# Mamba-2 scan and maxout FFN: seven products for block one's output, C of chunk two by VectorE, sign words by GpSimd, and a new order of the first steps

## The chip, the core and the metric

The kernel runs on one core of a Trainium2 chip. Its engines are TensorE (PE in the profile, its weight loads PEld), VectorE (DVE), ScalarE (ACT), GpSimd (POOL) and SyncE (SP), which issues the DMAs. Each works through its own queue in order; they wait for each other by semaphores. The metric is the device time of one execution in microseconds.

## What is computed

A Mamba-2 scan over 4 batches, 8 heads and 768 tokens (x of 32 per head, state of 16), whose output of 3072 tokens x 256 goes through a maxout feed-forward layer:

```python
for c in range(nc):                      # scan, per batch and head
    cum = np.cumsum(log(a[chunk]))
    L = np.exp(cum[:, None] - cum[None, :]) * causal
    y[chunk] = ((C @ B.T) * L) @ x + (C @ state) * np.exp(cum)[:, None]
    state = np.exp(cum[-1]) * state + (B * np.exp(cum[-1] - cum)[:, None]).T @ x
x = y.transpose(0, 2, 1, 3).reshape(3072, 256)
h = np.maximum(np.maximum(x @ w1, x @ w2), x @ w3)      # 256 x 768 each
out = h @ w_out                                         # 768 x 256
```

The weights come in float64, everything else in float32. The kernel uses chunks of 128 tokens where the reference has 32; the length of a chunk does not enter what is computed.

## The kernel before

**Blocks.** The 768 tokens are six chunks of 128. A chunk with its four batches makes a block of 512 token rows, c = 0 to 5. The text of the change counts from one: its block one is c = 0, its chunk three c = 2. For each block TensorE makes scores (C times B), VectorE multiplies them with the decays L, TensorE makes y from them and from the state, and the feed-forward layer follows.

**Feed-forward.** With w2 as base, h = x w2 + max(x(w1-w2), x(w3-w2), 0). The base part of the output is x G with G = w2 w_out, which is folded once (`fold_base`). For c > 0 the products of x with the weight differences, and those of h and x with w_out and G, are made by seven products in place of eight on halves of the operands (Strassen's way): `early_products` and `late_products` for the first, `down_seven` with `piece`, `first_four`, `all_seven` for the output. Seven products need sums and differences of the operands: of the weights (`weight_sums`, GpSimd), of y (`scan_sums`, VectorE), of h (`sums_of_h`, GpSimd, four instructions for a third of the rows), of w_out and G (`sums_of_out`, GpSimd). Block c = 0 uses plain products: `group` for x times the differences, `first_down` for the output, 16 steps of two matmuls 128x256. An fp32 matmul stands as two records in the profile.

**Weights.** Twelve pieces of 512 KB (nine of w1, w2, w3, three of w_out) are loaded as words of float64 and turned into float32 by hand. `decode_abs`: two ScalarE instructions, with the absolute value of the high words u put in SBUF ("dA") or in a PSUM bank ("dB"). `decode_bits`: three VectorE instructions (clamp L208, shift L211, join with the sign bit L213). `decode_sum`: GpSimd adds the low part (L220).

**Loads.** SP issues all large loads in the order of the steps. C of chunks three to five and B of the last are in `LONG`: eight loads of 32 KB with long runs, turned by four VectorE transposes (`turn_long`, L145) into SBUF. The other B and C are one load of 256 KB, turned by four TensorE transposes (L462) into a PSUM bank.

**Order.** `ORDER` is a list, written by hand, of named steps, up to the point where block c = 1 is nearly done; each engine gets its instructions in that order. After it a fixed plan (`STEADY`, `LAST`) runs blocks two to five. The names that matter here (c chunk, j piece, n and k counts):

- f: load of the next weight piece; lx, lB, lC, lL, lE: loads of x, B, C, L (half of the decays, 1 MB), E (eight rows); cs: store of the running sums; l3: all loads of chunk three
- dA, dB, dV, dP: decoding of piece j (ScalarE, VectorE, GpSimd); v: difference of weights (VectorE, L692); u: `weight_sums` (GpSimd)
- i, j, X: decays of chunk zero (TensorE, ScalarE); k, x: masks (GpSimd, L427) and exponentials (ScalarE, L434) of a later chunk; n, N: turning of sums to columns
- pB, pC: transposes of B, C; bB, c: copies of them (ScalarE); E, d: C times exp(cum), `scan_cd`; s: scores; w: scores times decays (VectorE, L556); o, y, Y: y from state, y from scores, copy; S: `scan_sums`; D, A, Z, z: the state
- g, G, H: x times the differences for block zero, and what follows; T, t, F, Fc: G folded
- e, ea, ev, K, Ko, Km, Kp: block one's (c = 1) early products, copy, sums, late products, their sums, maximum, `sums_of_h`
- O, Oc: `first_down`, and its copy and store; Sw, So: `sums_of_out` of w_out and of G

PSUM banks are shared: `att_bank` has four and takes every fifth from the one of sumA; `ffn_bank` has one and shares two of sumB. A step that asks for a bank waits until the last reader of the old content is through.

Of the kernel before, what the change touches and what calls it, by code (L numbers as in the profile page):

```python
# [19 lines left out]
def kernel(  # L20
# [20 lines left out]
    nc = tc.nc  # L41
# [3 lines left out]
    P = 128  # L45
# [76 lines left out]
    LONG = {(c, "C") for c in range(3, NC)} | {(NC - 1, "B")}  # L122
# [82 lines left out]
    def decode_bits(j):

        dst, hi, u, v, r = jobs[j]
        nc.vector.tensor_scalar(  # L208
            out=u.bitcast(FP32), in0=u.bitcast(FP32), scalar1=SMALL, scalar2=LARGE,
            op0=ALU.max, op1=ALU.min)  # L210
        nc.vector.tensor_scalar(  # L211
            out=u, in0=u, scalar1=3, scalar2=None, op0=ALU.logical_shift_left)
        nc.vector.scalar_tensor_tensor(  # L213
            out=v, in0=hi, scalar=0x80000000, in1=u,
            op0=ALU.bitwise_and, op1=ALU.bitwise_xor)

    def decode_sum(j):

        dst, hi, u, v, r = jobs[j]
        nc.gpsimd.tensor_tensor(  # L220
            out=dst.bitcast(U32), in0=v.rearrange("p (k f) -> p k f", k=2),
            in1=r.rearrange("p (k f) -> p k f", k=2), op=ALU.add)
# [706 lines left out]
    def down_seven(c, u, p):  # L929

        if p == EARLY[0]:
            open_seven(c, u, ffn_bank)
# [15 lines left out]
    def first_down(j):  # L948

        b, part = divmod(j, 4)  # L950
        u, i = divmod(b, 2)
        if j % 8 == 0:
            held["o"] = bank("ffn", 1, [P, 2, DM], "o")
        o = held["o"]
        for f in (2 * part, 2 * part + 1):
            if f < NF:
                one, two = hT[0][:, f, b * P:(b + 1) * P], wo_sb[:, f]
            else:
                one, two = yT[0][:, f - NF, b * P:(b + 1) * P], based["G"][:, f - NF]
            nc.tensor.matmul(  # L960
                out=o[:, i], lhsT=one, rhs=two, start=(f == 0), stop=(f == NF + KD - 1),
                skip_group_check=True)

    def first_out(u):
        ob = ffn.tile([P, 2, DM], FP32, tag="ob", bufs=2, name="ob")
        nc.scalar.copy(out=ob, in_=held["o"])
        nc.sync.dma_start(
            out=out.rearrange("(b s) m -> s b m", s=S)[0:P, 2 * u:2 * u + 2], in_=ob)
# [21 lines left out]

    step("tB", turn_rows, 0, "B")
# [16 lines left out]
    for c in range(3):  # L1008
        step("pB%d" % c, scan_tb, c, att_bank if c else pin("ffn"))
        step("bB%d" % c, scan_bt, c)  # L1010
        step("pC%d" % c, scan_tc, c, att_bank if c else pin("sumA"))
# [204 lines left out]
    for j in range(4 * NB):  # L1216
        step("O%d" % j, first_down, j)
    step("Oc0", first_out, 0)
    step("Oc1", first_out, 1)
# [4 lines left out]
        i0 ca fa tB pB0 bB0 tC j0 la X00 X01 ra pC0 c00 X11 f0 f1 lx0 f2 f3 c01 X10 s00 w001 w000  # L1224
        dA0 dA1 dV1 i2 j2 X20 dV0 n2 dP0 X21 s02 cs w002 w003 X31 f4 X30 w020 y00 Y00 w022 lB1 f5 f6
        n1 dP1 v0 g00 lL10 dA2 dB3 f7 f8 w021 w023 y02 Y02 dV2 f9 g10 dP2 lC1 lE1 N2 g01 H0 dV3 T0
        g11 dB4 lL12 dB5 dP3 v1 dV4 dV5 f10 f11 lx1 H1 t0 dP4 v2 pB1 N1 dB6 dB7 g20 g21 g30 dV6 D0
        lB2 fb bB1 dP5 k11 dP6 g31 G4 H3 H4 A0 G5 H2 dB8 H5 T1 t1 v3 n3 G6 G7 pC1 lC2 k10 x10 dV7
        dP7 dV8 v4 G8 H6 dP8 x11 N3 dA9 dV9 c10 E1 d1 G9 H7 Z0 H8 U k12 c11 s10 v5 x12 x13 G10 H9
        w100 dB10 w102 x14 dP9 w103 G11 s12 w101 k13 T2 x15 dV10 F0 u2 lL20 w120 D1 lE2 x16 x17 o1  # L1230
        w121 y10 y11 w122 alone u0 w123 y13 dP10 H10 u3 y12 A1 u5 u1 Y10 Y11 t2 H11 F1 S10 S11 S12
        S13 e0 lx2 pC2 Z1 ea0 ev0 pB2 dB11 K0 lL22 bB2 z1 dV11 dP11 Ko0 l3 c20 e1 ea1 ev1 O0 K1 E2
        k21 F2 Fc d2 Sw c21 Ko1 Km1 e2 k20 k23 ea2 O1 O2 ev2 K2 Ko2 s20 e3 x20 x21 k22 x22 x23 k30
        O3 O4 w203 O5 O6 O7 ea3 ev3 u4 w200 K3 x24 k31 x25 Oc0 Ko3 e4 ea4 So O8 Km3 O9 ev4 w201 O10
        K4 x30 x26 k33 Ko4 x27 O11 O12 w202 s22 w221 e5 w222 w223 w220 x31 x32 Kp1 x33 o2 y23 y20
        y21 y22 k32 Y20 Y21 S20 ea5 S21 O13 O14 O15 D2 ev5 Kp3 A2 Z2 K5 S22 S23 Ko5 x34 Oc1
# [125 lines left out]
```

## Time and profile before

| | |
|---|---|
| median of 3 runs | 256.97 us (256.96 to 257.55) |
| the profiled execution, whole | 257.36 us |
| its span in the profile | 255.6 us |
| granted TensorE clock | 0.999 |
| busy: PE, PEld, DVE, ACT, POOL | 247.3, 206.5, 172.7, 113.9, 107.2 us |
| read from and written to HBM | 24.54 MB, 3.24 MB |

The profile is one execution. Times of instructions count from the first one of the span. A PE record's end is modelled and overlaps the next one, so TensorE is read by the steps between starts. "<-" after an idle time names what ended it. In the table by stage each engine has its busy time and its count of instructions.

Landing times of loads, in us, as the issues of the trace have them: first two weight pieces 9.3 and 10.9, x of chunk zero 14.2, third piece 16.9; halves of L for chunk one 28.9 and 45.7; the eight rows E of chunk one 36.5 to 40.0; x of chunk one 52.0; C of chunk two 58.6.

### The profile page before, as it was taken

What the parts mean: (1) busy time and instruction counts of PE and PEld (TensorE: products, weight loads), DVE (VectorE), ACT (ScalarE), POOL (GpSimd) and SP (SyncE); (2) the same over time, 40 slices, a digit from 0 to 9 for tenths busy, and PEclk for the clock granted to TensorE, in tenths of its full rate; (3) what the DMA queues carried; (4) which work ended last, traced back from release to release, by engine and by line L of the source; (5) the groups of instructions that cost most, each with busy time, mean ns of one, the idle gap of its engine ahead of it and who ended that gap; (6) DMA issues with size and microseconds to landing.
All of it is one profiled execution on the core that took longest, in us unless ns stands there. A gap on an engine that the chain in (4) does not pass through costs nothing.

```text
span 255.6 us, 5657 instructions
## 1 busy us (share of the span) xinstructions
PE 247.3 (97%) x2172; PEld 206.5 (81%) x2172; DVE 172.7 (68%) x362; ACT 113.9 (45%) x308; POOL 107.2 (42%) x144
## 2 busy tenths in 40 slices
PE   8799899999999999999999999999999999999995
PEld 5357554588888887888899898898889899999994
DVE  4589998777627456588566688567877746645651
ACT  3837689845396844535164434354431211111010
POOL 2032682898949941661271470363230404134000
PEclk9999999999999999999999999999999999999999
DMA  3998968986995676868004925501000001001003
GB/s 107 240 295 235 344 88 205 232 99 178 199 299 130 93 109 169 234 81 137 4 0 129 256 62 97 80 3 41 3 13 29 3 0 44 0 3 41 1 15 110
DMA packets 85371, 28.16 MB, mean 110 GB/s; under 512 B 55392, under 2 KB 82016, under 8 KB 85344
## 3 DMA queue, kind: packets, MB, share of 16 engines
q1 hardware_dynamic: 84752, 27.40, 49.2%
q8 instruction: 17, 0.28, 0.5%
q10 hardware_dynamic: 592, 0.39, 0.5%
q14 instruction: 10, 0.08, 0.1%
HBM read 24.54 MB, written 3.24 MB: 109 GB/s over the span
## 4 chain that ended last, share of the span: by engine, by line
PE 82%; DVE 9%; issue 3%; POOL 2%; SPq 1%; DMA 1%; ACT 1%; POOLq 0%; DVEq 0%
PE o L886 25%; PE sumB L717 20%; PE sumA L717 16%; PE o L960 5%; PE s L548 5%; PE y L584 4%; PE fold L822 2%; PE y L571 2%; DVE w_u L213 2%; DVE u L211 2%; DVE u L208 1%; SPq L230 1%; DVE w L692 1%; DVE L L556 1%; DMA stage<-in_C_dram 1%
## 5 line engine op out<-in xcount | busy, mean ns | idle before, releaser
L434 ACT ACTIVATE L<-L,ncums 128x128 f32<-128x128 f32 x160 | 49.4, 392 | 3.4 <-POOL L L427 3.4
L556 DVE TENSOR_TENSOR L<-s,L 128x512 f32<-128x512 f32 x48 | 30.8, 682 | 10.6 <-ACT L L434 4.8
L717 PE MATMUL sumA<-yT,w 128*128 128x256 f32 x120 | 36.8, 388 | 0.0
L717 PE MATMUL sumB<-yT,rb 128*128 128x256 f32 x120 | 35.8, 380 | 0.0
L845 POOL TENSOR_TENSOR rb<-h 128x256 f32<-128x256 f32 x16 | 11.7, 730 | 56.9 <-DVE h L792 56.3
L745 ACT COPY eu<-sumA 128x256 f32<-128x256 f32 x30 | 11.2, 373 | 54.0 <-PE sumA L717 54.0
L427 POOL TENSOR_SCALAR_AFFINE_SELECT L<-L 128x1024 f32<-128x1024 f32 x20 | 21.6, 1092 | 9.1 <-DMA L<-cums 9.1
L717 PEld LDWEIGHTS sumB<-yT,rb 128*128 128x128 f32 x120 | 22.6, 190 | 3.5 <-issue 0.3
L656 PE MATMUL up<-yT,w 128*128 128x256 f32 (+1 forms) x64 | 23.0, 497 | 1.4 <-ACT yT L607 0.5
L717 PEld LDWEIGHTS sumA<-yT,w 128*128 128x128 f32 x120 | 19.4, 190 | 4.2 <-DVE rb L779 1.0
L755 DVE TENSOR_TENSOR eu<-sumA,eu 128x256 f32<-128x256 f32 x30 | 12.7, 422 | 13.7 <-ACT eu L745 13.6
L220 POOL TENSOR_TENSOR w<-w_u,w_r 128x512 uint32<-128x512 uint32 x9 | 12.5, 1392 | 20.6 <-DVE w_u L213 20.6
L845 POOL TENSOR_TENSOR w<-h 128x256 f32<-128x256 f32 x12 | 8.7, 729 | 28.0 <-DVE h L792 27.5
L656 PEld LDWEIGHTS up<-yT,w 128*128 128x128 f32 x64 | 11.3, 189 | 8.9 <-issue 5.3
L717 PE MATMUL sumA<-ys,rb 128*128 128x256 f32 x60 | 17.8, 379 | 0.0
L717 PE MATMUL sumB<-ys,w 128*128 128x256 f32 x60 | 17.8, 379 | 0.0
L717 PE MATMUL sumB<-ys,rb 128*128 128x256 f32 x60 | 17.8, 379 | 0.0
L548 PE MATMUL s<-CT,BT 32*128 32x256 f32 x192 | 15.8, 402 | 2.1 <-ACT CT L485 1.8
L886 PE MATMUL o<-rb,h 128*128 128x128 f32 x120 | 17.7, 275 | 0.0
L886 PE MATMUL o<-wo,h 128*128 128x128 f32 x120 | 17.6, 275 | 0.0
L779 DVE TENSOR_TENSOR m<-sumB,eu 128x512 f32<-128x512 f32 x15 | 10.3, 688 | 9.5 <-PE sumB L717 9.5
L548 PEld LDWEIGHTS s<-CT,BT 32*128 32x128 f32 x192 | 9.9, 184 | 7.2 <-ACT CT L485 2.8
(148 smaller groups left out, 516.2 us busy)
## 6 DMA issues: line engine op xcount, KB each, us to landing
L<-cums SPq DMA_DIRECT2D x10, 1024.0 KB, 8.8
rb<-in_moe_w_dram SPq DMA_DIRECT2D x9, 512.0 KB, 7.0
raw_x<-in_x_dram SPq DMA_DIRECT2D x6, 512.0 KB, 5.3
out_dram<-ob SPq DMA_DIRECT2D x10, 256.0 KB, 2.5
rb<-in_moe_w_out_dram SPq DMA_DIRECT2D x3, 512.0 KB, 8.3
E<-cums SPq DMA_DIRECT2D x40, 32.0 KB, 4.0
raw_B<-in_B_dram SPq DMA_DIRECT2D x4, 256.0 KB, 6.1
raw_C<-in_C_dram SPq DMA_DIRECT2D x24, 32.0 KB, 1.9
```

Source lines behind the costliest of these rows:

```text
L220: nc.gpsimd.tensor_tensor(out=dst.bitcast(U32), in0=v.rearrange("p (k f) -> p k f", k=2), in1=r.rearrange("p (k f) -> p k f", k=2), op=ALU ...
L427: nc.gpsimd.affine_select(out=Ls[c][:, b], in_=Ls[c][:, b], pattern=[[0, NH], [1, P]], compare_op=ALU.is_ge, fill=MASKED, base=0, channel_ ...
L434: nc.scalar.activation(L[:, b, h], L[:, b, h], AF.Exp, bias=ncum[c][:, b * NH + h:b * NH + h + 1], scale=1.0)
L548: nc.tensor.matmul(out=s[:, i].rearrange("j g i -> j (g i)"), lhsT=st["BT"][rows, b], rhs=st["CT"][rows, b].rearrange("p g i -> p (g i)"), ...
L556: nc.vector.tensor_tensor(out=M, in0=s, in1=M, op=ALU.mult)
L656: nc.tensor.matmul(out=bank[:, a:b], lhsT=w_sb[i][:, k, f * P:(f + 1) * P], rhs=yT[0][:, k, a:b], start=(k == 0), stop=(k == KD - 1), skip ...
L717: nc.tensor.matmul(out=bank[:, half], lhsT=left(p, k), rhs=sides[c][p], start=(first and half == 0), stop=True, skip_group_check=True)
L745: nc.scalar.copy(out=eu[:, 0], in_=units[c, k][0][:, 0])
L755: nc.vector.tensor_tensor(out=eu[:, 1], in0=A[:, 1], in1=eu[:, 0], op=ALU.add)
L845: eng.tensor_tensor(out=to, in0=a1, in1=a0, op=ALU.subtract)
L886: nc.tensor.matmul(out=o[SLOT[p]], lhsT=x[:, u * P:(u + 1) * P], rhs=right(p, pair), start=(p in opens and pair == 0), stop=True, skip_gro ...
L960: nc.tensor.matmul(out=o[:, i], lhsT=one, rhs=two, start=(f == 0), stop=(f == NF + KD - 1), skip_group_check=True)
```

## The change

1. `first_down` and `first_out` go. Block zero's output is made by `down_seven`, as that of the others: 14 steps O (two halves of the tokens, seven products each), the sums of y by the new `first_sums` (steps y0s, VectorE, in place in `yT[0]`), those of h by `sums_of_h` (steps h0 to h2, GpSimd). `first_four` and `all_seven` take the place of the copies Oc.
2. C of chunk two joins `LONG`; its four VectorE transposes are the steps pC2 and pD2, two each.
3. For pieces 3, 4, 6 and 10 (steps dC) GpSimd makes the sign word from the high words into v, and VectorE shifts u and joins it with v in one instruction. u of these is in PSUM. Piece 9 changes from dA to dB.
4. `ORDER` is another one: among others the second mask group stands ahead of the first scores; E of chunk one is loaded behind the second half of L; sums of weights (u) come in another order; A1 comes behind e1 and K1; no O step stands before K1.

```diff
@@ -10,6 +10,7 @@
 FP32 = mybir.dt.float32
 BF16 = mybir.dt.bfloat16
 U32 = mybir.dt.uint32
+I32 = mybir.dt.int32
 AF = mybir.ActivationFunctionType
 ALU = mybir.AluOpType
 AX = mybir.AxisListType
@@ -119,7 +120,7 @@
     blocks = {c: {} for c in range(NC)}
     sources = {"B": (B, N), "C": (C, N), "x": (x, D)}
 
-    LONG = {(c, "C") for c in range(3, NC)} | {(NC - 1, "B")}
+    LONG = {(c, "C") for c in range(2, NC)} | {(NC - 1, "B")}
 
     def load_long(c, name):
 
@@ -190,7 +191,7 @@
 
     jobs = {}
 
-    def decode_abs(j, beside):
+    def decode_abs(j, beside, sign=False):
 
         jobs[j] = dst, rb = fetched.pop(0)
         lo, hi = (rb.rearrange("p k f w -> p (k f) w")[:, :, i] for i in range(2))
@@ -200,14 +201,23 @@
         nc.scalar.activation(u.bitcast(FP32), hi.bitcast(FP32), AF.Abs)
         r = wtmp.tile(shape, U32, tag="w_r", bufs=2, name="w_r")
         nc.scalar.activation(r.bitcast(FP32), lo, AF.Copy, bias=2.0, scale=2.0 ** -51)
-        jobs[j] = dst, hi, u, v, r
+        if sign:
+            nc.gpsimd.tensor_scalar(
+                out=v.bitcast(I32), in0=hi.bitcast(I32), scalar1=0.0, scalar2=-2.0 ** 31,
+                op0=ALU.is_lt, op1=ALU.mult)
+        jobs[j] = dst, hi, u, v, r, sign
 
     def decode_bits(j):
 
-        dst, hi, u, v, r = jobs[j]
+        dst, hi, u, v, r, sign = jobs[j]
         nc.vector.tensor_scalar(
             out=u.bitcast(FP32), in0=u.bitcast(FP32), scalar1=SMALL, scalar2=LARGE,
             op0=ALU.max, op1=ALU.min)
+        if sign:
+            nc.vector.scalar_tensor_tensor(
+                out=v, in0=u, scalar=3, in1=v,
+                op0=ALU.logical_shift_left, op1=ALU.bitwise_xor)
+            return
         nc.vector.tensor_scalar(
             out=u, in0=u, scalar1=3, scalar2=None, op0=ALU.logical_shift_left)
         nc.vector.scalar_tensor_tensor(
@@ -216,7 +226,7 @@
 
     def decode_sum(j):
 
-        dst, hi, u, v, r = jobs[j]
+        dst, hi, u, v, r, sign = jobs[j]
         nc.gpsimd.tensor_tensor(
             out=dst.bitcast(U32), in0=v.rearrange("p (k f) -> p k f", k=2),
             in1=r.rearrange("p (k f) -> p k f", k=2), op=ALU.add)
@@ -926,10 +936,10 @@
 
     EARLY, LATE = (1, 7, 5, 6), (2, 4, 3)
 
-    def down_seven(c, u, p):
+    def down_seven(c, u, p, kind=ffn_bank):
 
         if p == EARLY[0]:
-            open_seven(c, u, ffn_bank)
+            open_seven(c, u, kind)
         piece(c, u, p, range(NQ + 1))
         if p == EARLY[-1]:
             first_four(c, u)
@@ -945,27 +955,21 @@
         c, j = downs.pop(0)
         down_seven(c, *j)
 
-    def first_down(j):
-
-        b, part = divmod(j, 4)
-        u, i = divmod(b, 2)
-        if j % 8 == 0:
-            held["o"] = bank("ffn", 1, [P, 2, DM], "o")
-        o = held["o"]
-        for f in (2 * part, 2 * part + 1):
-            if f < NF:
-                one, two = hT[0][:, f, b * P:(b + 1) * P], wo_sb[:, f]
-            else:
-                one, two = yT[0][:, f - NF, b * P:(b + 1) * P], based["G"][:, f - NF]
-            nc.tensor.matmul(
-                out=o[:, i], lhsT=one, rhs=two, start=(f == 0), stop=(f == NF + KD - 1),
-                skip_group_check=True)
-
-    def first_out(u):
-        ob = ffn.tile([P, 2, DM], FP32, tag="ob", bufs=2, name="ob")
-        nc.scalar.copy(out=ob, in_=held["o"])
-        nc.sync.dma_start(
-            out=out.rearrange("(b s) m -> s b m", s=S)[0:P, 2 * u:2 * u + 2], in_=ob)
+    def first_piece(j):
+
+        u, i = divmod(j, 7)
+        down_seven(0, u, (EARLY + LATE)[i], lambda shape, name: bank("ffn", 1, shape, name))
+
+    def first_sums(i):
+
+        y11, y12, y21, y22 = (
+            yT[0][:, k, r * HB:(r + 1) * HB] for k in range(2) for r in range(2))
+        if i == 0:
+            t = ffn.tile([P, 3, HB], FP32, tag="ys", bufs=3, name="ys")
+            sides[0] = {1: y11, 2: y21, 3: y22, 4: t[:, 2], 5: y12, 6: t[:, 0], 7: t[:, 1]}
+        t6, t7, t4 = sides[0][6], sides[0][7], sides[0][4]
+        to, a1, a0 = ((t7, y22, y12), (y12, y12, y11), (t6, y22, y12), (t4, y21, t6))[i]
+        nc.vector.tensor_tensor(out=to, in0=a1, in1=a0, op=ALU.subtract)
 
     last = []
 
@@ -988,6 +992,16 @@
         assert name not in steps, name
         steps[name] = lambda: fn(*args)
 
+    turned_c = {}
+
+    def turn_part(c, b):
+        if c not in turned_c:
+            turn_long(c, "C")
+            turned_c[c] = later[-NB:]
+            del later[-NB:]
+        for fn in turned_c[c][b:b + 2]:
+            fn()
+
     step("tB", turn_rows, 0, "B")
     step("tC", turn_rows, 1, "C")
     step("i0", spread_i, (0, 1))
@@ -1008,7 +1022,11 @@
     for c in range(3):
         step("pB%d" % c, scan_tb, c, att_bank if c else pin("ffn"))
         step("bB%d" % c, scan_bt, c)
-        step("pC%d" % c, scan_tc, c, att_bank if c else pin("sumA"))
+        if (c, "C") in LONG:
+            step("pC%d" % c, turn_part, c, 0)
+            step("pD%d" % c, turn_part, c, 2)
+        else:
+            step("pC%d" % c, scan_tc, c, att_bank if c else pin("sumA"))
         step("c%d0" % c, scan_c, c, (0,), None if c else nc.vector)
         step("c%d1" % c, scan_c, c, (1,))
 
@@ -1072,6 +1090,7 @@
     for j in range(12):
         step("dA%d" % j, decode_abs, j, False)
         step("dB%d" % j, decode_abs, j, True)
+        step("dC%d" % j, decode_abs, j, True, True)
         step("dV%d" % j, decode_bits, j)
         step("dP%d" % j, decode_sum, j)
 
@@ -1213,27 +1232,29 @@
     for q in range(NQ):
         step("F%d" % q, fold_base, q)
     step("Fc", lambda: nc.scalar.copy(out=based["G"], in_=based["sum"]))
-    for j in range(4 * NB):
-        step("O%d" % j, first_down, j)
-    step("Oc0", first_out, 0)
-    step("Oc1", first_out, 1)
+    for j in range(14):
+        step("O%d" % j, first_piece, j)
+    for i in range(4):
+        step("y0s%d" % i, first_sums, i)
+    for q in range(NQ):
+        step("h%d" % q, sums_of_h, 0, q)
     step("Sw", sums_of_out, "wo")
     step("So", sums_of_out, "G")
 
     ORDER = """
-        i0 ca fa tB pB0 bB0 tC j0 la X00 X01 ra pC0 c00 X11 f0 f1 lx0 f2 f3 c01 X10 s00 w001 w000
-        dA0 dA1 dV1 i2 j2 X20 dV0 n2 dP0 X21 s02 cs w002 w003 X31 f4 X30 w020 y00 Y00 w022 lB1 f5 f6
-        n1 dP1 v0 g00 lL10 dA2 dB3 f7 f8 w021 w023 y02 Y02 dV2 f9 g10 dP2 lC1 lE1 N2 g01 H0 dV3 T0
-        g11 dB4 lL12 dB5 dP3 v1 dV4 dV5 f10 f11 lx1 H1 t0 dP4 v2 pB1 N1 dB6 dB7 g20 g21 g30 dV6 D0
-        lB2 fb bB1 dP5 k11 dP6 g31 G4 H3 H4 A0 G5 H2 dB8 H5 T1 t1 v3 n3 G6 G7 pC1 lC2 k10 x10 dV7
-        dP7 dV8 v4 G8 H6 dP8 x11 N3 dA9 dV9 c10 E1 d1 G9 H7 Z0 H8 U k12 c11 s10 v5 x12 x13 G10 H9
-        w100 dB10 w102 x14 dP9 w103 G11 s12 w101 k13 T2 x15 dV10 F0 u2 lL20 w120 D1 lE2 x16 x17 o1
-        w121 y10 y11 w122 alone u0 w123 y13 dP10 H10 u3 y12 A1 u5 u1 Y10 Y11 t2 H11 F1 S10 S11 S12
-        S13 e0 lx2 pC2 Z1 ea0 ev0 pB2 dB11 K0 lL22 bB2 z1 dV11 dP11 Ko0 l3 c20 e1 ea1 ev1 O0 K1 E2
-        k21 F2 Fc d2 Sw c21 Ko1 Km1 e2 k20 k23 ea2 O1 O2 ev2 K2 Ko2 s20 e3 x20 x21 k22 x22 x23 k30
-        O3 O4 w203 O5 O6 O7 ea3 ev3 u4 w200 K3 x24 k31 x25 Oc0 Ko3 e4 ea4 So O8 Km3 O9 ev4 w201 O10
-        K4 x30 x26 k33 Ko4 x27 O11 O12 w202 s22 w221 e5 w222 w223 w220 x31 x32 Kp1 x33 o2 y23 y20
-        y21 y22 k32 Y20 Y21 S20 ea5 S21 O13 O14 O15 D2 ev5 Kp3 A2 Z2 K5 S22 S23 Ko5 x34 Oc1
+        i0 tB ca la pB0 bB0 f0 f1 j0 X01 X11 tC f2 pC0 c00 c01 dA0 X00 i2 lx0 f3 j2 X10 s00 dA1 dV0
+        ra dV1 dP1 w000 w001 fa n1 X20 w003 f4 f5 cs w002 s02 dP0 v0 f6 X21 X30 X31 w023 N1 y00 Y00
+        g00 w022 dA2 dC3 w020 w021 lB1 dV2 T0 t0 f7 lL10 f8 f9 y02 lC1 lL12 Y02 dC4 g10 dB5 dV3 dV4
+        dP2 v1 g01 H0 g11 dV5 dP3 dP4 H1 lE1 g20 pB1 g21 g31 f10 dC6 dV6 v2 H2 dB7 g30 H3 lx1 dP5 v3
+        T1 t1 G4 G5 f11 dP6 D0 A0 bB1 k11 dV7 Z0 n2 N2 U H4 dB8 G6 dV8 dP7 v4 k10 u0 H5 dP8 fb n3 H6
+        G7 G8 dB9 pC1 G9 lB2 T2 dV9 H7 v5 N3 x10 u2 x11 x12 H8 c10 c11 s10 x13 w102 w100 k12 G10 G11
+        w103 H9 y0s0 x14 E1 s12 w101 H10 k13 x15 d1 u1 lL20 lC2 w120 w121 dP9 dC10 dV10 D1 x16 o1
+        dP10 x17 w122 dB11 y10 F0 w123 y12 y13 dV11 y11 Y10 Y11 S10 alone F1 h0 dP11 u3 h1 k21 H11
+        t2 S11 S12 S13 e0 ea0 ev0 lL22 y0s1 y0s2 K0 pB2 Ko0 e1 ea1 lx2 pC2 pD2 c20 F2 Fc k20 x20 Sw
+        c21 ev1 So K1 Ko1 A1 e2 ea2 Z1 bB2 s20 x21 h2 k23 Km1 ev2 x22 x23 w203 w200 z1 y0s3 O0 K2
+        lE2 l3 k22 O1 O2 Ko2 O3 e3 ea3 w201 u4 ev3 O4 O5 K3 Ko3 w202 x24 O6 e4 ea4 Km3 s22 ev4 O7 O8
+        k30 x25 k33 E2 d2 x26 x30 x27 w223 u5 k32 K4 Ko4 w220 O9 O10 w222 w221 e5 o2 k31 y20 D2 ea5
+        ev5 y21 x31 x32 x33 y23 Kp1 y22 Y20 Y21 O11 S20 S21 O12 O13 A2 Kp3 Z2 S22 K5 S23 Ko5 x34
     """
 
     for word in ORDER.split():
```

## The prediction

> **What bounds the kernel now.** I read four views: the busy table by stage, the chain of waits, the groups by line and shape, and the timelines. Stages first (per engine busy us, then clock, DMA share, GB/s):
>
> ```profile
> 12.00:30.00 18.00, 16.64 (x168) 11.60 (x167) 16.94 (x30) 11.69 (x21) 6.63 (x5) 1.00 1.08 276
> 30.00:57.00 27.00, 25.98 (x254) 15.37 (x255) 23.47 (x42) 20.79 (x54) 19.96 (x25) 1.00 0.92 170
> 57.00:103.00 46.00, 45.96 (x353) 38.46 (x352) 26.37 (x51) 26.71 (x79) 31.45 (x43) 1.00 0.82 171
> 103.00:239.00 136.00, 136.00 (x1207) 122.39 (x1206) 92.95 (x207) 46.31 (x136) 47.59 (x62) 1.00 0.26 57
> ```
>
> The reader is to see two regimes. From 57 us (step e0) TensorE never rests, at full clock: a microsecond of its work removed there is a microsecond of time. Before, VectorE is the full one (16.9 of 18), and TensorE's gaps can be won. The chain of waits says what fills VectorE:
>
> ```profile
> 24.82 0.60 DVE w L692
> 25.42 0.62 DVE u L208
> 26.07 0.71 DVE u L211
> 26.80 0.69 DVE w_u L213
> ...
> 57.26 0.86 PE sumA L717 x4
> ...
> 68.67 1.73 PE o L960 x8
> ```
>
> Weight pieces in three VectorE instructions each (L208, L211, L213), a difference (L692), then from 57 us only TensorE, block one's output (L960) among it. Prices come from the groups (count | busy us, mean ns | idle before):
>
> ```profile
> L960 PE MATMUL o<-wo,h 128*128 128x256 f32 x48 | 11.4, 381 | 0.0
> L886 PE MATMUL o<-wo,h 128*128 128x128 f32 x120 | 17.6, 275 | 0.0
> L211 DVE TENSOR_SCALAR u<-u 128x512 uint32<-128x512 uint32 x8 | 5.6, 699 | 0.3
> L845 POOL TENSOR_TENSOR rb<-h 128x256 f32<-128x256 f32 x16 | 11.7, 730 | 56.9 <-DVE h L792 56.3
> L462 PE MATMUL trC<-ident,raw_C 128*128 128x128 f32 x12 | 1.9, 277 | 0.2 <-DVE raw_C L239 0.2
> ```
>
> Matmuls overlap, so I price them by their pace in the chain: 8 of L960 take 1.73 us, 0.216 each; 120 of L886 took 13.41 us, 0.112 each.
>
> **The change, part by part.**
>
> *Products.* Before: 64 records of L960 x 0.216 = 13.8 us. After: 2 halves x 7 products x 4 pairs x 2 passes = 112 records x 0.112 = 12.5. **-1.3 us**, all in the saturated stretch.
>
> *C of chunk two.* Four TensorE transposes (0.43 us in the chain, "PE trC L462 x4" at 58.99 took 0.44) go: **-0.44**. VectorE gets four of L145 (1.15 us for four at 103.73); it has 20 us idle of 46 there: nothing. If that cover were gone, s20 would wait 1.2 us. SP issues eight 32 KB loads for one of 256 KB; eight issues of about 0.47 us are 3.7, the one it replaces held SP 3.9 (49.71 to 53.59): nothing.
>
> *Side work of the seven products.* VectorE: four differences (0.42 each) and ten small additions (0.29): 4.6 us; ScalarE: four copies of 0.27 for two of 0.59: nothing. In the idle just named. GpSimd: 12 of L845 at a step of 0.8 (83.36 to 86.46 holds four): **9.6 us**, and this isn't hidden for certain, see below.
>
> *Sign words.* Four pieces (3, 4, 6, 10) lose L211 (0.70 and its gap), piece 9 goes from the cheap form (0.43 + 0.43 + 0.69) to the PSUM form (0.70 + 0.71 + 0.69): 4 x 0.72 - 0.55 = 2.3 us off VectorE, of which one early y difference takes 0.42 back. The GpSimd sign instruction is in no row. Low end: half of a 1024-wide mask (L427, 1.09), 0.55; high end the longest L220, 1.72. I take 0.7, since it has one input like the mask. Pieces 3, 4 and 6 fall where GpSimd has 11 us idle in 18; what waits behind signs 3 and 4 in its queue is dP2, and v1 behind dP2; by the queues below dP2 has 1.5 us to spare, so even 1.4 each costs little.
>
> *Order, to e0.* I put the new queues together by hand from these rows. (a) TensorE's second mask group (i2, j2: 2.9 us) now fills the hole ahead of s00 (8.84 to 10.39), and ScalarE's last exponentials end at 15.5, not 17.0: s02 ends near 16.2 (18.1), y00 starts near 16.9, held by x of chunk zero, which SP now sends behind a third weight piece (landing 14.2 before; by 16.9 after, when both had landed). g00 at 18.8 (19.9). (b) VectorE from dV0 (10.5) to v5 sums to 30.2 us and about 1 us of waits: v5 at 41.6 against 43.8. But v1, v2 come at 25.0, 29.1 (25.4, 30.1), since dV4 to dV6 now stand ahead of them; G4 starts at 29.8 (30.3). (c) From G4 TensorE's 16.7 us to G11 run through: 46.5 (47.9). (d) SP sends the second half of L for chunk one ahead of eight E rows: before it was issued at 38.2 and landed at 45.7, and GpSimd's masks waited 5.6 us for it; now near 41, and x of chunk one at about 46 to 50 (52.0). (e) Then ScalarE's exponentials set the pace: 15.2 us from 34.6 to the last of chunk one, 49.5 to 50.5 (52.9); o1 waits for a bank freed by w121, 49.1; the y's end near 53.7, fold F1 fills 1.7, **e0 at 55.6 (57.1): -1.5**. Bounds: 54.4, where o1 and the loads wait for nothing, and 57.0, where x or the piece in the last buffer lands as late as before. A1 (0.56) has moved behind e0: **+0.56**.
>
> *Order, after e0.* K0 follows e0 directly. Before, two transposes (0.87) stood between; the first additions (L755 to L757) ended 2.9 us after e0 began and e0 lasts 1.73: K0's second product waits: **+0.9**. Bounds 0 (if e0 itself is held by its own y differences) and 1.2.
>
> *GpSimd's queue.* It runs full from about 47. Piece 11 is added near 56.0; then u3 1.84, block-one differences h1 3.2, two masks 2.13, Sw 4.7 (64.47 to 69.17 before), So 2.5, h2 3.2 with its first result after 0.8: 71.2; its end 73.6; mask, state, mask, u4: 79.0. TensorE reaches the last part of O1, which reads h2, at 55.6 + 15.4 = 71.0, and e4, which reads u4, at 78.7. **+0.3**, taken at e4. Bounds: 0, if GpSimd is 1 us earlier, and +3.2, if O1 waits for all of h2 (73.6 against 70.4).
>
> One row speaks of a longer queue:
>
> ```profile
> 24.74 0.68 DVE L692 TENSOR_TENSOR w<-w,w 128x512 f32<-128x512 f32 x1
> ...
> 24.97 1.59 POOL L220 TENSOR_TENSOR w<-w_u,w_r 128x512 uint32<-128x512 uint32 x1 [1.06 <-DVE w_u L213]
> 27.63 1.27 POOL L220 TENSOR_TENSOR w<-w_u,w_r 128x512 uint32<-128x512 uint32 x1 [1.07 <-DVE w_u L213]
> ```
>
> The addition that meets a VectorE instruction with both inputs in SBUF takes 0.32 us more. The Trainium skill (SBUF — State Buffer, section "SBUF: two separate sides") has this as a rule: such a VectorE instruction and a GpSimd one take turns at a shared port pair, for the whole instruction. By it the y differences (both inputs in SBUF) could each stop GpSimd for their 0.42, 1.3 us on this queue for the three after e0. The trace agrees in kind. The sum would then stand 1.3 us higher.
>
> *Sum:* -1.3 - 0.44 - 1.5 + 0.56 + 0.9 + 0.3 = **-1.5 us**. Its base is the profiled execution, 257.36 (span 255.6 and 1.8 around it); that is 0.4 above the median 256.97, and I carry the difference over: **255.5**.
>
> **Rivals.**
>
> *The new order comes out cleaner* (e0 at 54.4, no wait at K0 or e4): -1.3 - 0.44 - 2.7 + 0.56 = -3.9, at most; about 253.5 as its middle. For it: ScalarE, VectorE and the loads all end earlier by my sums. Against: each gain runs into the next engine's queue.
>
> *The front gains nothing* (e0 at 57.0, for example if SP's blocked issues, which before held f2 from 6.9 to 11.95, hold other loads now): -1.3 - 0.44 + 0.56 + 0.9 = -0.3: 256.7. For it: loads are full to 57 us (share 0.92 and above). Against: VectorE's 2.3 us are off for certain.
>
> *GpSimd becomes the bound; slower.* Place: the stretch from piece 11 to u4, 23 us without a gap, against TensorE's 23.1 from e0 to e4. Each microsecond that it is longer, TensorE waits at O1, O2 or e4. From 2.3 us more the gain is eaten. O1 waiting for the whole of h2 takes 3.2 in place of 0.3 (-1.5 + 2.9 = +1.4); so do eight collisions of 0.3 to 0.45. About 258.1. For it: L845's differences went nearly without a wait behind them before (idle 56.9 for h) and now stand ahead of needed work. Against: the pieces of h2 are separate instructions, and O1 needs only the first.
>
> *The change doesn't do what it says:* the signs come late, and VectorE waits for GpSimd at dV3, dV4: then v1 is late by as much, at most 1.4: 256.9, in with the second rival.
>
> **How the numbers follow.** What can be told from no change is 0.3%, 0.8 us. Forecast 0.42, of its own 254.7 to 256.2; cleaner 0.21; front gains nothing 0.14; GpSimd bound 0.23. Faster: forecast and cleaner, 0.63, less a little at the edge: 0.62; same 0.15; slower 0.23. Range 252.8 to 258.2: below it only the cleaner case's best quarter, above it the GpSimd case beyond 3 us of wait.
>
> **What would show it.** Right: 112 records of o at 0.112 between e0 and 103 us, no L960; the first L717 at 54.4 to 57; a TensorE gap of about 0.9 inside the second group of L717; GpSimd without idle from 47 to 79; pieces 3, 4, 6 and 10 with two VectorE instructions of 0.69. Wrong: TensorE idle of more than 1 us at o, released by POOL L845 or L705 (the slower rival); e0 after 57; a sign instruction above 1.7 us; TensorE gaps after 103 us, where I see no reason for any.

## The result, and the profile after

| | before | after |
|---|---|---|
| median | 256.99 us (256.86 to 257.55, 6 runs) | 258.55 us (258.52 to 258.91, 6 runs) |
| ratio | | 1.0058, interval 1.0045 to 1.0071 |
| the profiled execution, whole; its span | 257.36; 255.6 | 258.55; 256.8 |
| first product of G4 | 30.30 | 31.48 (forecast 29.8) |
| end of G11 | 47.89 | 48.72 (46.5) |
| e0 | 57.10 | 58.13 (55.6) |
| start of the next block's products | 98.46 | 99.59 |

The kernel became slower by 0.6%, where 255.5 us was forecast. Line numbers have moved: the sign is L205, VectorE's clamp, join with the sign word, shift and old join are L213, L217, L221, L223, GpSimd's addition L230, the difference of weights L702, the maxima H L1162, the sums of h L855, `piece` L896.

The stages of the changed kernel (span, then busy us and count of PE, PEld, DVE, ACT, POOL, then clock, DMA share, GB/s):

```profile
12.00:30.00 18.00, 14.40 (x167) 11.01 (x162) 16.87 (x30) 12.76 (x25) 13.72 (x9) 1.00 1.10 256
30.00:57.00 27.00, 25.18 (x221) 14.00 (x220) 23.41 (x38) 21.07 (x55) 24.48 (x29) 1.00 0.96 207
57.00:103.00 46.00, 45.33 (x428) 38.85 (x428) 31.61 (x70) 25.75 (x80) 38.09 (x51) 1.00 0.67 142
```

From 12 to 30 us GpSimd has 13.7 us of work where it had 6.6, and VectorE is as full as before (16.87 and 16.94). The chain that ended last, followed back from e0, tells what that did:

```profile
7.42 11.07 DMA rb<-in_moe_w_dram
...
18.65 1.21 POOL w_u L205
...
20.58 2.04 POOL w_u L205
...
25.52 1.58 POOL w L230
27.10 1.95 POOL w_u L205
29.07 0.69 DVE w_u L217
29.76 1.06 DVE w L702
30.82 0.61 DVE h L1162
31.48 3.70 PE up L666 x8
```

Before, this stretch of the chain was VectorE's three instructions for each piece. Now it is GpSimd's: its signs stand in it three times, the last directly ahead of VectorE's join (L217), the difference v2 (L702), a maximum (L1162) and G4. The groups give the price (count | busy us, mean ns | idle before):

```profile
L205 POOL TENSOR_SCALAR w_u<-rb 128x512 int32<-128x512 int32 x4 | 8.1, 2046 | 1.2 <-DMA rb<-in_moe_w_dram 1.2
L217 DVE SCALAR_TENSOR_TENSOR w_u<-u,w_u 128x512 uint32<-128x512 uint32 x4 | 2.8, 692 | 0.7 <-POOL w_u L205 0.4
L896 PE MATMUL o<-wo,h 128*128 128x128 f32 x144 | 21.0, 275 | 0.0
```

A sign takes 1.95 to 2.3 us; the prediction had 0.7. The products did what was forecast: all output products are L896 now, 672 in place of 560 and 64 of the old form, at 0.111 us each. GpSimd's timeline (start, us, then operation, tiles, count, and the idle time before the first in brackets) shows where the time was taken:

```profile
18.65 4.22 POOL L205 TENSOR_SCALAR w_u<-rb 128x512 int32<-128x512 int32 x2 [1.24 <-DMA rb<-in_moe_w_dram]
22.81 4.29 POOL L230 TENSOR_TENSOR w<-w_u,w_r 128x512 uint32<-128x512 uint32 x3
27.06 1.97 POOL L205 TENSOR_SCALAR w_u<-rb 128x512 int32<-128x512 int32 x1
29.01 2.95 POOL L230 TENSOR_TENSOR w<-w_u,w_r 128x512 uint32<-128x512 uint32 x2
```

From 18.65 to 34.5 us GpSimd has no idle time. And after e0 the step K0 waits as forecast (TensorE's timeline):

```profile
59.42 0.59 PE L727 MATMUL sumB<-ys,rb 128*128 128x256 f32 x2
60.08 0.70 PE L727 MATMUL sumA<-yT,w 128*128 128x256 f32 x2
61.09 0.70 PE L727 MATMUL sumB<-yT,rb 128*128 128x256 f32 x2 [0.32 <-DVE m L767]
```

Two matmuls take 0.43 us, so the first start is 0.22 late and the second 0.58: 0.8 us.

Each run below had the kernel before beside it on the same chip; on these chips a part of the runs had a granted clock of 0.985 to 0.993, which lifts the medians of before to between 257.4 and 258.3, so lowest times (before: 256.8 to 257.0) are given where medians mislead.

### The profile page after: what moved, and what is told of

It reads as the page before. It is cut to its first block, busy times and chain, and to the rows that moved or that the text cites. A ratio compares the mean times of both kernels' runs of the same rounds, so it can differ in the third digit from the quotient of the medians.

```text
span 256.8 us, 5797 instructions
## 1 busy us (share of the span) xinstructions
PE 244.4 (95%) x2216; PEld 205.6 (80%) x2216; DVE 178.3 (69%) x376; ACT 113.8 (44%) x310; POOL 126.0 (49%) x160
## 4 chain that ended last, share of the span: by engine, by line
PE 84%; DMA 4%; POOL 4%; DVE 3%; SPq 2%; issue 1%; ACT 1%; POOLq 0%; DVEq 0%
PE o L896 30%; PE sumB L727 19%; PE sumA L727 15%; PE up L666 6%; DMA rb<-in_moe_w_dram 4%; PE s L558 4%; PE y L594 4%; PE fold L832 2%; PE y L581 2%; POOL w_u L205 2%; POOL w L230 2%; SPq L240 1%; PE A L521 1%; SPq L189 1%; PE trB L472 1%
## 5 line engine op out<-in xcount | busy, mean ns | idle before, releaser
L855 POOL TENSOR_TENSOR rb<-h 128x256 f32<-128x256 f32 x22 | 16.1, 734 | 57.2 <-DVE h L802 56.3
L855 POOL TENSOR_TENSOR w<-h 128x256 f32<-128x256 f32 x12 | 8.8, 730 | 28.3 <-DVE h L802 27.8
L437 POOL TENSOR_SCALAR_AFFINE_SELECT L<-L 128x1024 f32<-128x1024 f32 x20 | 22.6, 1147 | 0.0
L896 PE MATMUL o<-wo,h 128*128 128x128 f32 x144 | 21.0, 275 | 0.0
L896 PE MATMUL o<-rb,h 128*128 128x128 f32 x144 | 21.0, 275 | 0.0
L230 POOL TENSOR_TENSOR w<-w_u,w_r 128x512 uint32<-128x512 uint32 x9 | 12.1, 1358 | 13.8 <-ACT L L391 12.4
L896 PE MATMUL o<-rb,yT 128*128 128x128 f32 x96 | 18.8, 278 | 0.0
L896 PEld LDWEIGHTS o<-wo,h 128*128 128x128 f32 x144 | 18.5, 192 | 0.0
L896 PEld LDWEIGHTS o<-rb,h 128*128 128x128 f32 x144 | 18.5, 192 | 0.0
L896 PEld LDWEIGHTS o<-rb,yT 128*128 128x128 f32 x96 | 16.5, 191 | 2.2 <-issue 0.5
```

The lines of the kernel that those rows point to most:

```text
L230: nc.gpsimd.tensor_tensor(out=dst.bitcast(U32), in0=v.rearrange("p (k f) -> p k f", k=2), in1=r.rearrange("p (k f) -> p k f", k=2), op=ALU ...
L437: nc.gpsimd.affine_select(out=Ls[c][:, b], in_=Ls[c][:, b], pattern=[[0, NH], [1, P]], compare_op=ALU.is_ge, fill=MASKED, base=0, channel_ ...
L855: eng.tensor_tensor(out=to, in0=a1, in1=a0, op=ALU.subtract)
L896: nc.tensor.matmul(out=o[SLOT[p]], lhsT=x[:, u * P:(u + 1) * P], rhs=right(p, pair), start=(p in opens and pair == 0), stop=True, skip_gro ...
```

## The experiments

**no_sign: the four pieces decoded by VectorE alone, in the new order.**

```diff
-dC3 ... dC4 ... dC6 ... dC10
+dB3 ... dB4 ... dB6 ... dB10
```

> The changed kernel with pieces 3, 4, 6 and 10 decoded as before (three VectorE instructions, no sign word on GpSimd), all else as changed. Theory A (the sign instruction, 1.95 to 2.1 us each in the changed trace where 0.7 was taken, fills GpSimd from 18.7 to 31 us and delays v1, v2 and G4): GpSimd's additions of pieces 2 to 5 come 4 us earlier, VectorE pays 4 x 0.72 = 2.9 us back; G4 near 30.5 (31.5 changed, 30.3 before), e0 near 57.0 (58.1 changed), time 257.0 to 257.8. Theory B (the new order is slow by itself, for example x of chunk zero behind a third weight piece, and the signs cost nothing): VectorE's 2.9 us more come on top, e0 at 59.5 or later, time 259.5 or more.

Measured: 260.66 us (lowest 259.91), ratio 1.009, interval 1.0061 to 1.012; e0 at 59.55. That is slower than the changed kernel, and both marks are those of theory B. VectorE stood without a gap ahead of the differences: v1 came at 26.25 (25.29 in the changed kernel), G4 at 32.38. So the new order needs the relief, as B says; that the signs cost nothing, B's other half, doesn't follow, since the work of the signs went to VectorE here (sign_free, below, finds a cost).

**sign_alone: the sign words of the same four pieces, in the kernel before.**

```diff
-dB3 ... dB4 ... dB6 ... dB10        (order of the kernel before)
+dC3 ... dC4 ... dC6 ... dC10
```

> The kernel before with nothing but the sign words of pieces 3, 4, 6 and 10 made by GpSimd, at the same places in the old order. Theory A: VectorE saves 2.9 us but waits for GpSimd, whose queue there has some 11 us of 18 idle; the four instructions take 2 us each, and the additions behind them come late; time 257.0 to 259. Theory B (signs harmless, VectorE relieved, order at fault): 255.5 to 256.5.

Measured: 259.09 us, ratio 1.0037, interval 1.0005 to 1.0069; lowest 258.28, 1.5 us above the lowest of before. In the old order too the signs take more than they give, at 1.96 to 2.0 us each. Where they take it, the trace does not show: it is 1.53 us late already at s02 (17.13 for 15.60), ahead of the first sign at 19.4, with a granted clock of 0.83 from 8 to 12 us and 0.74 from 12 to 16, and e0 is no later than that (58.63 for 57.10).

**sign_free: the changed kernel with the sign instructions left out** (the join reads a column of zeros, so the four pieces' weights are all positive; all else is computed).

```diff
-        if sign:
-            nc.gpsimd.tensor_scalar(out=v..., in0=hi..., op0=ALU.is_lt, op1=ALU.mult)
...
-                out=v, in0=u, scalar=3, in1=v,
+                out=v, in0=u, scalar=3, in1=no_sign.to_broadcast([P, 2 * WCOL]),
```

> The changed kernel without the four sign instructions; VectorE's join reads a column of zeros in place of the sign words, so the signs of four weight pieces are left out. It shows the order and VectorE's relief with signs at no cost on GpSimd. Theory A (the size of the sign instruction is what failed in the prediction): v1 at 25.0, G4 near 30, e0 at 55.6 to 56.5, time 256.2 to 257.0. Theory C (the order holds the front back by itself, whatever the signs cost, since dV4 to dV6 stand ahead of v1 and v2 and the copies and banks behind them come late): e0 at 57.3 or later, time 257.8 or more.

Measured: 257.26 us, ratio 0.9988, interval 0.996 to 1.0016: 1.29 us below the changed kernel. G4 starts at 30.14 and e0 at 56.77, 1.34 and 1.36 earlier. This is the cost of the four signs, with VectorE's relief kept. Time and e0 lie between the two theories: the signs are a part of the miss, the order another. GpSimd's timeline shows where the signs had stood:

```profile
22.26 4.29 POOL L226 TENSOR_TENSOR w<-w_u,w_r 128x512 uint32<-128x512 uint32 x3 [4.88 <-DVE w_u L219]
27.63 2.99 POOL L226 TENSOR_TENSOR w<-w_u,w_r 128x512 uint32<-128x512 uint32 x2 [1.08 <-DVE w_u L219]
```

Signs 3 and 4 fell into 4.88 us of idle time and moved the additions behind them from 22.26 to 22.81. Sign 6 fell into 1.08 us, and the next additions went from 27.63 to 29.01. What this did to G4 stands in VectorE's queue. The changed kernel:

```profile
21.00 0.84 DVE L221 TENSOR_SCALAR w_u<-w_u 128x512 uint32<-128x512 uint32 x1
29.07 0.69 DVE L217 SCALAR_TENSOR_TENSOR w_u<-u,w_u 128x512 uint32<-128x512 uint32 x1 [0.42 <-POOL w_u L205]
29.68 1.15 DVE L702 TENSOR_TENSOR w<-w,w 128x512 f32<-128x512 f32 x1
```

and the same three instructions in sign_free:

```profile
20.96 0.43 DVE L217 TENSOR_SCALAR w_u<-w_u 128x512 uint32<-128x512 uint32 x1
28.20 0.69 DVE L213 SCALAR_TENSOR_TENSOR w_u<-u,no_sign 128x512 uint32<-128x512 uint32 x1
28.80 0.68 DVE L700 TENSOR_TENSOR w<-w,w 128x512 f32<-128x512 f32 x1
```

The shift of piece 2 took 0.41 longer while sign 4 ran (20.58 to 22.87), the join of piece 6 waited 0.32 longer, for sign 6, and v2 took 0.47 longer while a GpSimd addition ran. That makes 1.20 of the 1.34; the rest is small gaps. The addition of piece 2 was not it: it ended at 24.1, and v1 started at 25.29 without a wait.

Even free signs leave the kernel no faster than before, so 0.7 us each could not have given 255.5.

**k0_cover: two steps of TensorE put between e0 and K0.**

```diff
-e0 ea0 ev0 lL22 y0s1 y0s2 K0 pB2 Ko0 ... K1 Ko1 A1 e2
+e0 ea0 ev0 lL22 y0s1 y0s2 pB2 A1 K0 Ko0 ... K1 Ko1 e2
```

> The changed kernel with pB2 and A1 (0.44 and 0.56 us of TensorE) moved ahead of K0, nothing else. If the gaps of 0.2 and 0.6 us at K0 are TensorE time lost for good: 257.7 (0.8 less than 258.55). If another queue (GpSimd's sums for O1 and e4, which ended 0.3 us ahead of TensorE) takes the place: 258.2 to 258.6.

Measured: 257.76 us (lowest 257.66), ratio 1.0005, interval 0.9971 to 1.0038: 0.8 us below the changed kernel, as the first of the two says. The wait was real and on the path. **no_sign_k0**, the same in no_sign:

> Both edits: no sign words, and pB2 and A1 ahead of K0. Theory A: the two gains add, 256.2 to 257.0, which is at or a little below the kernel before. Theory B: 258.7 or more.

259.88 us, ratio 1.0049, interval 1.0016 to 1.0083; lowest 259.14 against 259.91: 0.8 again, and theory B, as in no_sign.

**sign_f32: the sign reads its words as float32.**

```diff
-                out=v.bitcast(I32), in0=hi.bitcast(I32), ...
+                out=v.bitcast(I32), in0=hi.bitcast(FP32), ...
```

> The changed kernel with the sign instruction reading the same words as float32 instead of int32; the sign and the result are the same. If turning int32 into numbers makes the 1.95 us: 0.6 to 1.2 us each, e0 1 us earlier, time near 257.5. If it is the strided read (every second word) or the int32 result: 1.95 us again and 258.5.

258.48 us, the instruction 1.97: the source type is not the price. **sign_forms** gave each of the four pieces another form:

> The changed kernel with four forms of the sign instruction, one in each of the four pieces (three of them give wrong signs, so only their durations are read): piece 3 with a contiguous source of two operations, piece 4 with the strided source and one operation, piece 6 with a contiguous float32 source and float32 result, piece 10 as it was. Theory A (the strided read, every other word, costs the time): pieces 3 and 6 at 0.7 to 1.3 us, pieces 4 and 10 at 1.95. Theory B (two operations in software): piece 4 at about 1.0, the others 1.95. Theory C (the int32 result): piece 6 alone short. Theory D (this instruction has this price on this engine whatever the form): all at 1.8 to 2.1.

```profile
L206 POOL TENSOR_SCALAR w_u<-w_r x1: 2087/2087/2087, 21.1 to 21.1; 128x512 int32<-128x512 int32 x1
L210 POOL TENSOR_SCALAR w_u<-rb x1: 1534/1534/1534, 23.2 to 23.2; 128x512 int32<-128x512 int32 x1
L214 POOL TENSOR_SCALAR w_u<-w_r x1: 1926/1926/1926, 30.1 to 30.1; 128x512 f32<-128x512 f32 x1
L218 POOL TENSOR_SCALAR w_u<-rb x1: 1950/1950/1950, 52.0 to 52.0; 128x512 int32<-128x512 int32 x1
```

Lines are, from the top: contiguous source; one operation; contiguous source and float32 throughout; unchanged (min, median, max ns; each form ran once). Neither a contiguous source nor float32 helps; one operation less takes 0.42 off. A and C fall, B holds for part of it, D for most.

**old_front and old_front_L: the old order up to e0, without the signs, and the new products behind it.** The second also issues the second half of L ahead of the E rows.

> The order of the kernel before up to the last y sum ahead of e0 (without A1 and u5, with h0 in GpSimd's old wait for L and h1 behind u1), pieces decoded as before, and from e0 on the changed kernel's steps with pB2 and A1 ahead of K0: seven products and the C of chunk two kept, signs and new front order undone. If the new front is what loses: e0 at 56.5 (57.1 less A1), time 255.4 to 256.2, under the kernel before. If the rest of the change loses as well (GpSimd's sums late for O1 or e4): 256.8 or more, with TensorE gaps at o.

> The same, and the second half of L for chunk one loaded ahead of the eight E rows, the one move of the new front that the changed trace bears out (landing at 40.6, not 45.7). If GpSimd's masks held chunk one's y back before: another 0.3 to 1.0 us less than the kernel above, 254.8 to 255.8. If not: the same time, since TensorE's queue and ScalarE's exponentials set e0.

263.27 and 263.1 us, ratios 1.0216 (1.0155 to 1.0277) and 1.0227 (1.0133 to 1.032). They settle nothing about the front, for two reasons. The granted clock of all eight executions was 0.986 to 0.993 (in old_front's trace 0.57 from 12 to 16 us). And the joining of the two halves put three y differences and the transposes of C ahead of block one's second sums on VectorE; TensorE waited 2.33 us for them at K1:

```profile
69.59 0.78 PE L727 MATMUL sumA<-yT,w 128*128 128x256 f32 x2 [2.33 <-DVE eu L765]
```

**v_first: v1 and v2 ahead of decodes on VectorE**, with the cover of K0.

```diff
-dV3 dV4 dP2 v1 g01 ... dC6 dV6 v2 H2 dB7 g30 H3
+dV3 dP2 v1 dV4 g01 ... dC6 v2 dV6 H2 dB7 g30 H3
```

> The changed kernel with the K0 cover (run k0_cover, 257.76) and two swaps on VectorE's queue: the difference v1 ahead of the decode of piece 4, and v2 ahead of the join of piece 6, which waits for the slow sign. Theory A (G4 was late only because v2 stood behind that join, 29.63 where its own inputs were there at 27.1): first product of G4 at 29.4 to 30.0 (31.43 before the swaps), e0 at 56.3 to 56.9 (58.09), time 256.0 to 256.6. Rival B (GpSimd's queue as a whole, four signs of 1.95 us and all additions, sets the pace up to 45 us, so that what is won at G4 is lost at v3 to v5 or at the masks): G4 may come earlier, but e0 at 57.6 or later, time 257.3 to 257.8.

257.02 us (lowest 256.83), ratio 0.9985, interval 0.9956 to 1.0015: 0.74 below k0_cover, half of what A forecast. G4 came at 30.55, e0 at 57.19, between the two theories. VectorE's timeline names the next in the queue:

```profile
27.81 0.68 DVE L702 TENSOR_TENSOR w<-w,w 128x512 f32<-128x512 f32 x1
28.41 0.69 DVE L213 TENSOR_SCALAR u<-u 128x512 f32<-128x512 f32 x1
29.20 0.69 DVE L217 SCALAR_TENSOR_TENSOR w_u<-u,w_u 128x512 uint32<-128x512 uint32 x1
29.81 1.27 DVE L1162 TENSOR_TENSOR h<-m,up 128x512 f32<-128x512 f32 x2
```

v2 starts at 27.81 (29.68 in the changed kernel), but H2 and H3 still stand behind piece 6, and TensorE waited 1.25 us for them.

**h_first: H2 and H3 ahead of it as well.**

```diff
-dC6 v2 dV6 H2 dB7 g30 H3 lx1
+dC6 v2 H2 g30 H3 dV6 dB7 lx1
```

> v_first (257.02), with the two maxima H2 and H3 also ahead of piece 6's decode on VectorE (in v_first they stood behind it, 29.81, and G4 waited 1.25 us for them). Theory A (the rest of G4's lateness is this queue): first product of G4 at 29.1 to 29.9 (30.55), e0 at 55.9 to 56.6 (57.19), time 255.8 to 256.4. Rival B (the additions of pieces 5 to 8, shifted by the signs, come to the front): G4 early, but e0 above 57.0 and time within 0.2 of v_first.

256.73 us, ratio 0.9972, interval 0.9947 to 0.9997. G4 came at 29.39, as A said, but e0 only at 57.11, as B said; the time is 0.29 below v_first, where B allows 0.2. TensorE's timeline shows where it was given back, GpSimd's and VectorE's why:

```profile
29.39 3.69 PE L666 MATMUL up<-yT,w 128*128 128x512 f32 x8
34.13 0.65 PE L521 MATMUL A<-raw_x,Bd 128*32 128x64 f32 x32 [1.05 <-POOL Bd L511]
```

```profile
29.39 1.28 POOL L230 TENSOR_TENSOR w<-w_u,w_r 128x512 uint32<-128x512 uint32 x1
31.48 1.58 POOL L230 TENSOR_TENSOR w<-w_u,w_r 128x512 uint32<-128x512 uint32 x1 [0.81 <-ACT w_r L203]
33.02 1.06 POOL L511 TENSOR_TENSOR Bd<-raw_B,from_j 128x512 f32<-128x512 f32 x1
```

```profile
30.64 0.69 DVE L217 SCALAR_TENSOR_TENSOR w_u<-u,w_u 128x512 uint32<-128x512 uint32 x1
```

The state product needs Bd, and Bd stood behind the addition of piece 6, which waited. The view names ScalarE (w_r) for this wait, and so does the next expectation, but the w_r that ended just then (30.70, 0.68 us) is piece 7's; piece 6's was written from 28.00 to 28.69. What came last for piece 6 is VectorE's join, from 30.64 to 31.33, and h_first itself had put it behind H2 and H3: in v_first it started at 29.20, and the addition did not wait. So the cause is neither that of A nor that of B, but the edit's own other side.

**d0_first: Bd ahead of that addition.**

```diff
-G4 G5 f11 dP6 D0 A0
+G4 G5 f11 D0 dP6 A0
```

> h_first (256.73), with GpSimd's state product Bd of chunk zero ahead of piece 6's addition: in h_first that addition stood idle 0.81 us for ScalarE's copy and Bd behind it let TensorE's state product wait 1.05 us. Theory A (what h_first won at G4 was lost at this one wait): no wait there, e0 at 55.9 to 56.3 (57.11), time 255.5 to 255.9, faster than the kernel before by 1 us or more. Rival B (the additions of pieces 6 to 8 now come late, v4, or the masks of chunk one): TensorE waits elsewhere before 48 us, e0 at 56.8 or later, time within 0.3 of h_first.

**255.95 us** (255.85 to 257.14), ratio 0.9933, interval 0.991 to 0.9956: faster than both kernels, 1.0 us below the median of before on the first chip and 2.6 below the changed kernel (which did not run on this chip). A holds, with the time 0.05 above its range:

```profile
29.22 3.70 PE L666 MATMUL up<-yT,w 128*128 128x512 f32 x8
32.85 0.65 PE L521 MATMUL A<-raw_x,Bd 128*32 128x64 f32 x32
...
56.23 0.59 PE L727 MATMUL sumA<-yT,w 128*128 128x256 f32 x2
```

**v_first_d1 and h_first_f0: the wait of o1 for its bank.** In the changed kernel TensorE waits 0.86 us after s12 for a bank. Both runs put the fold F0 there (v_first_d1 also takes d1 earlier; h_first_f0 also takes the last exponentials and masks ahead of piece 10's decode).

```diff
-w121 dP9 dC10 dV10 D1 x16 o1 dP10 x17 w122 dB11 y10 F0 w123
+w121 dP9 F0 dC10 dV10 D1 x16 o1 dP10 x17 w122 dB11 y10 w123          (v_first_d1)
+x16 x17 ... w121 dP9 F0 dC10 w122 w123 dV10 D1 o1 dP10 dB11 y10      (h_first_f0)
```

> v_first, and in the stretch of 46 to 58 us the product d1 (which frees the bank that piece 10's magnitude waits 1.48 us for) taken ahead of the block-one difference, and the first fold F0 put between s12 and o1, where TensorE waited 0.86 and 0.16 us for VectorE's masks. Theory A (those waits are the rest of what the front lost): another 0.8 to 1.1 us, e0 at 55.3 to 56.0, time 255.1 to 255.8, faster than the kernel before by 1 us or more. Rival B (the exponentials of the second half end last and y waits for them wherever F0 stands): within 0.3 us of v_first.

> h_first, and the first fold F0 between s12 and o1 once more, now with the exponentials x16 and x17 and their masks ahead of piece 10's decode. Moving F0 hands it the bank that piece 10's magnitude had, and every later taker the next bank of the ring. Theory A (v_first_d1 was slow because the shifted ring let o1 wait for the last masks, which stood behind the decode of piece 10): with the masks early the order gains, o1 at 49.5 to 50.5, e0 0.5 to 1.0 us earlier than in h_first, time 255.0 to 255.8. Rival B (the place of F0 itself, or the earlier C difference, was the fault): o1 again after 52, time at 257.5 or more.

260.21 us (lowest 258.48; ratio 1.0084, interval 1.0049 to 1.0119) and 257.96 (1.001, 0.998 to 1.004). F0 takes a bank of the ring, so everything behind it got the next one: in v_first_d1 o1 waited for the last masks, 2.33 us. (Its trace has a granted clock of 0.92 from 30 to 58 us, so its e0, 61.57, can't be compared.) With the masks early (h_first_f0) this wait is gone, as A said, o1 follows F0 without a gap, but F1 then waits 0.44 us for piece 10 and e0 0.67 for the y differences. From the end of G11 to e0 it took 9.28 us (48.98 to 58.26) where h_first took 9.40: a gain of 0.1 where A forecast 0.5 to 1.0. By its time, h_first_f0 is where rival B put it (257.5 or more).

Where h_first_f0 lost is shown for its profiled execution alone, which took 259.23 us, 2.44 more than that of h_first. 1.28 us were gone at v1, ahead of the moved steps, to a collision (last section). From e0 to the next block's products it took 42.04 us (40.74 in h_first), with waits of 0.78 at s20 for ScalarE's copy of B and 0.46 at an O step for a sum of h. Eight of the twelve executions took 257.85 to 258.02 and four, this one among them, 259.08 to 259.35; so most of them probably have only one of the two losses, and which one is open.

## Why the prediction was wrong

The forecast for e0 was 55.6; it came at 58.13. With the marks of the prediction:

| stretch | forecast | measured | miss |
|---|---|---|---|
| start of G4 | 29.8 | 31.48 | 1.7, of which the signs 1.34 (sign_free) |
| G4 to the end of G11 | 16.7 | 17.24 | 0.5 |
| end of G11 to e0 | 9.1 | 9.41 | 0.3 |

- **Sign words: the first step that failed.** The price was taken as 0.7 us between 0.55 and 1.72, "since it has one input like the mask"; it is 1.95 to 2.3, above both ends. In the sum the signs stand at nothing ("even 1.4 each costs little"); they cost 1.34 us at G4 and 1.36 at e0 (sign_free). The reasoning looked only at what waits behind signs 3 and 4 in GpSimd's queue, the addition of piece 2, and there it was right: that addition held nothing up. It did not ask what a GpSimd instruction of 2 us does to VectorE's instructions beside it (0.41 at piece 2's shift), nor what stands behind sign 6: two additions in GpSimd's queue, one of which lengthened v2 by 0.47, and in VectorE's the join, and behind the join v2, H2 and H3, for which G4 waits.
- **Order, to e0: the second.** Its -1.5 came as -0.33 even with free signs (e0 at 56.77 in sign_free, 57.10 before), although A1, 0.56 us, had left this stretch. (a) g00 was forecast at 18.8 and came at 18.88. (b) v1 ended at 25.97 for 25.0, v2 at 30.83 for 29.1, v5 at 43.33 for 41.6. Without signs G4 still stands at 30.14. "dV4 to dV6 now stand ahead of them" was in the text, and G4 was still put 0.5 earlier than before; taking v1, v2, H2 and H3 ahead of them and Bd ahead of an addition moved e0 by 1.84 us (58.07 in k0_cover to 56.23 in d0_first), with the signs in place. This queue order, not the sum over VectorE's work, was what set G4. (c) The stretch G4 to G11 has no wait of note in the changed kernel and took 17.24, as in k0_cover and v_first; the 16.7 is a sum of TensorE's own work that came out 0.5 too small. (d) Loads came as forecast: the second half of L at 40.6 (41), x at 48.3 (46 to 50). (e) The 0.3 hides two misses. o1 waited for its bank, but less than forecast: it came 2.0 us behind the end of G11, for 2.6. From o1 to e0 TensorE ran with no wait but one of 0.17 and took 7.4 us for 6.5. So TensorE's own work set e0 here, and not ScalarE's exponentials. Without VectorE's relief the new order is slower up to e0 than the old one: 59.55 for 57.10 (no_sign).
- **K0: right.** 0.9 forecast, 0.8 in the trace, 0.8 by k0_cover.
- **Products and C: right, their sum in part by luck.** From e0 to the next block's products 41.36 us before; the terms -1.3, -0.44, +0.56, +0.9, +0.3 make 41.38; measured 41.46. But the +0.3 at e4 did not come. Without it the sum is 0.38 short, and other small losses fill this: the next block's first product, for one, started 0.38 behind the end of the one ahead of it, where it was 0.21 before.
- **GpSimd's queue after e0: right that it runs full, and it costs nothing.** The first result of h2 came at 73.04 and O1's use at 73.37; u4 ended at 80.92 and e4 started at 81.75. Nor did the 1.3 us of collisions that the prediction set beside its sum show as a wait on this queue.
- **The base.** The profiled execution of before lay 0.4 above its median, that of after on its median: 0.4 of the 3.05 us that the forecast is off; 2.5 come from e0 (1.36 of them the signs, 1.17 the order) and 0.1 from what follows it.
- **The rivals.** "GpSimd becomes the bound" had the engine right and the place wrong: it named 56 to 79 us, it was 18 to 31. That its 258.1 lies near 258.55 is chance (its own +1.4 would make it 258.4). "Signs come late" had the mechanism, VectorE held up by GpSimd, and with "at most 1.4" nearly the size; it named waits at dV3 and dV4, and it was piece 2's shift, dV6 and v2. Its 256.9 counts neither the missing gain of the order nor the wait at K0.

What the trace after should show was put down well: "a sign instruction above 1.7 us" and "e0 after 57" were the marks of a wrong forecast, and both are there.

## What to carry to other kernels

Work moved to an idle engine is priced per instruction by that engine's own rows of the same operation; where there is none, the range must reach well beyond the nearest row, and every one of the moved instructions needs its own line for what stands behind it in both queues. A sum over an engine's work shows that it could finish earlier, not that the one instruction TensorE waits for does: here four short edits of the hand-written order (k0_cover, v_first, h_first, d0_first) turned 0.6% slower into 0.7% faster (0.9933), with the slow sign instruction kept. A move also puts something else later, as h_first did with the join of piece 6, and that instruction's followers need the same look. And a step that takes a buffer from a ring moves every later taker by one, so it must not be moved as if it were free.

## What the runs showed of the hardware

The two-operation comparison of 512 columns on GpSimd takes 1.95 us, more than the addition of two inputs of that size (1.27) and as much as 1.8 masks of 1024 (1.09 each); of the forms tried, only the one with a single operation was clearly shorter (1.53, one instruction). VectorE's shift of the same size with one input, in SBUF, took 0.43 us, and 0.84 beside such a comparison.

VectorE's difference of weights, both inputs in SBUF, took 0.68 us alone and up to 1.82 when it met an addition of GpSimd. VectorE's timeline of h_first_f0:

```profile
24.20 1.82 DVE L702 TENSOR_TENSOR w<-w,w 128x512 f32<-128x512 f32 x1 [0.15 <-POOL w L230]
```

0.69 of it is its own; 1.13 is about the rest of a GpSimd addition that ran at the same time. In h_first the same difference started first, at 24.05, and took 0.69, and the addition, from 24.14, took 1.73 instead of 1.27. The prediction had only this second way round, GpSimd's addition longer by 0.3. The Trainium skill (SBUF — State Buffer, section "Who interferes with whom") says that the order of issue decides which of the two is blocked; these two traces agree. Of the changed kernel's six differences three took 0.95 to 1.58 us. TensorE waited for two of the six: for v1, and, through the maximum behind it, for v2.
